# A spectral filter's rows dealt over other partitions, with a divided first load and copies made by DMA, in a one-core GFNet and GEGLU kernel

## The chip, the core and the metric

The kernel runs on one core of a Trainium2 chip. The metric is the device time of one execution in microseconds (us), the median of a few runs. Before the change it is 485.1 us (three runs, 485.1 to 485.33).

## The reference

What is computed is one block of a network: a layernorm, a filter in the frequency domain (GFNet) with a residual, a second layernorm, and a gated feed-forward part with a residual. Sequence 2048, features 576, hidden width 4608, all inputs bf16.

```python
def _A_ref(x, w_r, w_i):                      # x: 1 x 2048 x 576
    X = jnp.fft.rfft2(x.astype(jnp.float32), axes=(-2, -1))
    X = X * (w_r + 1j * w_i)                  # w_r, w_i: 2048 x 289
    return jnp.fft.irfft2(X, s=(S, D), axes=(-2, -1)).astype(jnp.bfloat16)

def _B_ref(x, w_gate, w_up, w_down):
    return (_gelu(x @ w_gate) * (x @ w_up)) @ w_down

h = x + _A_ref(_layernorm(x), A_w_r, A_w_i)
h2 = h + _B_ref(_layernorm(h), B_w_gate, B_w_up, B_w_down)
```

The change is in how the filter `w_r + 1j * w_i` gets into the on-chip memory (SBUF).

## The kernel before, in words

All matmuls are on TensorE (PE). VectorE (DVE) and ScalarE (ACT) move results out of PSUM and do the elementwise work, GpSimd (POOL) and SyncE (SP) issue DMA transfers; POOL does some elementwise work too. The order of each engine's instructions is written out by hand in strings (`SEQ1`, `SEQF`, `SEQ`), and a small scheduler (`Prog`) puts a semaphore wait in front of an instruction for each thing that it reads or overwrites. Each engine works through its own list in order.

The stages, with the times of the profiled execution:

- **Up to about 19 us**: x is loaded (2304 KB), normalised, and taken through a first DFT over 128 of the 2048 positions (`a_mm`, L551).
- **The filter stage, about 19 to 44 us** (`SEQF`). The spectrum is worked on in 16 steps i = 0 to 15; step i has the filter group `GORD[i]` = 1, 2, ... 15, 0. For each step: `D`/`d` is a DFT over the features (L640), moved out as tile `CUS`; `B` a DFT over 16 positions (L660), moved out as `YS` (there are three `YS` buffers); `T` (`st_T`, L673) multiplies `YS` with the filter tile `WS`, two DVE instructions to `TP` and `TR`; `V`/`v` and `R`/`r` (L681, L698) are the first inverse DFT, moved out as `V` and `RB`, and `RB` is spread into `VR` by small DMAs. The list begins `D2 D0 d2 D1 d0 d1 B2 D5 B0 d5 T2 D3 B1 d3 D4 T0 T1 B5 d4 D8 ...`. DVE makes the moves of `d1`, `d8`, `B1` and `B7`, ACT the other moves of `d` and `B`. So DVE's own order here is d1, T2, B1, T0, T1, d8, T3, T5, T4, T6, ...
- **About 43 to 55 us** (`SEQ`): the rest of the inverse transform (`I`, L835 and `N`, L852), the residual and the second layernorm.
- **From there to the end**: the feed-forward part, which is matmuls back to back (L944 and L1044).

**The filter tile.** `WS` is 128 partitions x 2 halves `jp` x 2 planes `pl` (0: w_r, 1: w_i) x 16 groups x 289 values. Half `jp` is loaded from HBM into the 64 partitions from 64·jp on alone: 32 of them hold "up" rows and 32 hold "down" rows (the mirrored frequencies, whose group order is reversed). Then the same 64 rows are copied to the other 64 partitions (`dup_w`), so that every partition has both halves. `st_T` of a step waits for these copies: `dup[0]` for steps 0 to 4, `dup[1]` for steps 5 to 7, `dup[2]` for steps 8 to 11, `dup[3]` from step 12 on.

- `w_up(pl, hf)` (L449) loads the up rows of a plane: two DMAs (jp = 0, 1) of 32 partitions, each row one run. `hf` 0 is groups 0 to 8 (162.6 KB a DMA), `hf` 1 groups 9 to 15 (126.4 KB).
- `w_down(pl, hf, sls, eng, sem)` (L456) loads the down rows: four DMAs (sl = 0 to 3) of 16 partitions, in runs of 578 bytes (72.2 or 63.2 KB each).
- `w_zero(pl)` (L464) loads group 0 of the down rows, two DMAs of 18.1 KB.
- SP issues, in this order: the loads of x and of tables, then for plane 1 and then plane 0 `w_up` and `w_down` of half 0 (12 DMAs), the table `VT`, the same for half 1, except that the last two `w_down` of plane 0 are issued by POOL, then `w_zero`.
- `dup_w(k, jp, pl, eng)` (L719) copies. k = 0 is groups 1 to 5, k = 1 groups 6 to 8, k = 2 groups 9 to 12, k = 3 groups 13 to 15 and 0. For k = 0, plane 1 is copied by two POOL instructions (L730) and plane 0 by two DVE instructions (L728); the others are DMAs which POOL issues. Copies of k = 0 and 1 wait for the loads of half 0, those of k = 2 and 3 for half 1.
- After the last copy SP loads the tables `VT2`, `DT`, `IT` (`tab_load`), and after them some of the `VR` pieces.
- The tables `BTAB` and `VTAB` (L140 to L152) hold the DFT coefficients in the same order of rows as `WS`; q there is the partition within a half, `half` is up or down, `r` the row, `sl` the slot.

Of the kernel before, what the change touches and what calls it, by code (L numbers as in the profile page):

```python
# [7 lines left out]
ALU = mybir.AluOpType  # L8

S, D, K2 = 2048, 576, 289  # L10
# [5 lines left out]
NT = 16  # L16
# [30 lines left out]
def build_tables():  # L47
# [52 lines left out]
    for st in range(2):  # L100
        g = 1 - st
        for p in range(128):
            half, r, jj = p // 64, (p % 64) // 4, p % 4
            low = (g + 16 * jj) if half == 0 else _minus_rows(g)[jj]
            k = 128 * r + low
            w = np.exp(-2j * np.pi * ((k * nn) % 2048) / 2048.0)
            if low in (0, 64):
                sl, ri = 0, (0 if low == 0 else 1)
# [8 lines left out]
            if half == 0:  # L117
                sl = jj
                e = np.exp(-2j * np.pi * ((r * nn) % 16) / 16.0)
                ca, cb = e, 1j * e  # L120
            else:
                sl = (128 - low - g) // 16
# [17 lines left out]
    for st in range(2):  # L140
        for jp in range(2):
            for q in range(64):
                half, r, sl = q // 32, (q % 32) // 2, 2 * jp + q % 2
                jj = sl if half == 0 else (4 - sl) % 4 if st else 3 - sl
                po, cut = 64 * half + 4 * r + jj, slice(2 * jp, 2 * jp + 2)
                for m in range(2):
                    for ri in range(2):
                        BN[jp, :, :, st, m, ri, q] = B[st, m + ri, :, cut, :, po].reshape(16, 4)
                for ri in range(2):
                    VN[st, jp, ri, q, 0] = V[st, ri, po, :, :, cut].reshape(2, 16, 4)  # L150
                    VN[st, jp, ri, q, 1] = (1 - 2 * ri) * V[st, 1 - ri, po, :, :, cut].reshape(2, 16, 4)
# [7 lines left out]
    a = np.full((K2 - 1, 1), 2.0)  # L159
# [172 lines left out]
def _build(nc, A_x, A_w_r, A_w_i, B_w_gate, B_w_up, B_w_down, out):  # L332
    P = Prog(nc)
    T = build_tables()
    dram = {n: nc.inline_tensor(_np_bf16(T[n]), name="c_" + n.lower()) for n in T}
    PE, DVE, ACT, SP, POOL = "pe", "dve", "act", "sp", "pool"
# [12 lines left out]
    WS = sb.alloc("WS", [128, 2, 2, NG, K2], BF16)  # L349
# [54 lines left out]
    ATS = sb.alloc("ATS", [128, NT, 128], BF16)  # L404
# [41 lines left out]
    P.dma(SP, FT[:, :, :].rearrange("p a b -> p (a b)"), dram["FTAB"][:, :], "ft", w=["FT"])  # L446
    P.dma(SP, BT[:, :, :, :].rearrange("p a b c -> p (a b c)"), dram["BTAB"][:, :], "bt", w=["BT", "BT1"])

    def w_up(pl, hf):  # L449
        g0, g1 = ((0, 9), (9, 16))[hf]  # L450
        src = (A_w_r, A_w_i)[pl].tensor
        for jp in range(2):
            P.dma(SP, WS[64 * jp:64 * jp + 32, jp, pl, g0:g1, :].rearrange("p g k -> p (g k)"),
                  bass.AP(src, (32 * jp + g0) * K2, [[128 * K2, 16], [16 * K2, 2], [1, (g1 - g0) * K2]]), f"w{pl}{hf}", w=[("W", hf, pl, jp)])

    def w_down(pl, hf, sls=(0, 1, 2, 3), eng=SP, sem=""):  # L456
        g0, g1 = ((1, 9), (9, 16))[hf]
        src = (A_w_r, A_w_i)[pl].tensor
        for sl in sls:
            p0 = 64 * (sl // 2) + 32  # L460
            P.dma(eng, WS[p0 + sl % 2:p0 + 32:2, sl // 2, pl, g0:g1, :], bass.AP(src, (64 + 16 * (3 - sl) + 16 - g0) * K2, [[128 * K2, 16], [-K2, g1 - g0], [1, K2]]),
                  f"w{pl}{hf}{sem}", w=[("W", hf, pl, 2 + sl)])

    def w_zero(pl):  # L464
        for jp in range(2):
            P.dma(SP, WS[64 * jp + 32:64 * jp + 64, jp, pl, 0, :], bass.AP((A_w_r, A_w_i)[pl].tensor, (64 + 32 * jp) * K2, [[128 * K2, 16], [(-16 if jp else 48) * K2, 2], [1, K2]]),
                  f"wz{pl}", w=[("W", 2, pl, jp)])

    for pl in (1, 0):
        w_up(pl, 0)  # L470
        w_down(pl, 0)
    P.dma(SP, VT[:, 0:2, :, :].rearrange("p a b c -> p (a b c)"), dram["VTAB"][:, 0:512], "vt", w=["VT", "VT1"])
    for pl in (1, 0):
        w_up(pl, 1)
        w_down(pl, 1, (0, 1, 2, 3) if pl else (0, 1))
    for pl in (1, 0):
        w_zero(pl)
    GORD = list(range(1, NG)) + [0]
    wkeys = [[("W", hf, pl, h) for pl in range(2) for h in range(6 if hf < 2 else 2)] for hf in range(3)]

# [98 lines left out]
    for w in SEQ1:  # L581
        a = w[1:]
# [9 lines left out]
    for t, w in enumerate(SEQF):  # L592
        k, i = w[0], w[1:].rstrip("abc")
        if k in "DBVR":
            b = min((b for b in used if b not in busy), key=lambda b: used[b])
# [4 lines left out]
        elif k in "dvr":  # L600
            b = FB[k.upper(), int(i)]
# [16 lines left out]
                op = mm(h, o, seqs[h][j], not second and j == 0, second and j == len(seqs[0]) - 1, [prev[o]] if second and j == 0 else [])  # L618
                turn_over.setdefault(key, [None, None])[o] = op

    dup = [[("Wd", 0, jp, pl, 1) for jp in range(2) for pl in range(2)]] + [[("Wd", k, jp, 0, g) for jp in range(2) for g in ((6,), (9,), (13, 0))[k - 1]] for k in range(1, 4)]

    wdv = B_w_down[:, :].rearrange("(c p) d -> p c d", p=128)

# [91 lines left out]
                src = PS[32 * j:32 * j + 32, b0 * 512:(b0 + 2) * 512].rearrange("p (a c) -> p a c", a=2)[:, :, 128 * (i == LAST) + 64 * t_:128 * (i == LAST) + 64 * t_ + 64]  # L716
                ev((ACT, DVE, DVE, ACT)[j], dst, src, keys, [("V", g, 2 + t_)])

    def dup_w(k, jp, pl=slice(0, 2), eng=None):  # L719
        a, b = 64 * jp, 64 - 64 * jp  # L720
        n = ("Wd", k, jp, pl.start)
        for g0, g1 in (((1, 6),), ((6, 9),), ((9, 13),), ((13, 16), (0, 1)))[k]:
            dst, src = (WS[q:q + 64, jp, pl, g0:g1, :].rearrange("p a g k -> p a (g k)")[:, :, 1:] for q in (b, a))
            r = [x for x in (wkeys[1] if g0 > 8 else wkeys[0] if g0 else wkeys[0] + wkeys[2]) if pl.start <= x[2] < pl.stop]
            if eng is None:
                op = P.dma(POOL, dst, src, f"wd{k}{jp}", r=r, w=[(*n, g0)])
            elif eng == DVE:
                P.op(DVE, lambda v: v.tensor_copy(dst, src), r=r, w=[(*n, g0)])  # L728
            else:
                P.op(POOL, lambda v: v.tensor_scalar(dst, src, 1.0, 1.0, op0=ALU.mult, op1=ALU.mult), r=r + [("ATS", NT - 1)], w=[(*n, g0)])  # L730
        return op if eng is None else None

    w_down(0, 1, (2, 3), POOL, "p")
    for jp in range(2):
        dup_w(0, jp, slice(1, 2), POOL)
        dup_w(0, jp, slice(0, 1), DVE)
    for jp in range(2):
        dup_w(1, jp)
    c = 0
    while c < NT:  # L740
        c1 = c + 1
        while c not in ACT_TILES and c1 < NT and c1 not in ACT_TILES:
            c1 += 1
        src, f, keys = (SA[:, 0, c:c1], -1.0 / D, "SA0") if c in ACT_TILES else (MV1[:, c:c1, 0], -1.0, "MV1")
        P.op(POOL, lambda g, c=c, c1=c1, src=src, f=f: g.tensor_scalar(NM[:, c:c1], src, f, 1.0, op0=ALU.mult, op1=ALU.mult),
             r=[(keys, k) for k in range(c, c1)], w=[("NM", k) for k in range(c, c1)])
        c = c1
    for k in (2, 3):
        for jp in range(2):
            last = dup_w(k, jp)  # L750
    def hold(eng=SP):
        P.op(eng, None, after=[P.ops[PE][-1]])

# [55 lines left out]
    SLOT, last, held, ing = {}, [sorted(used.values()).index(used[2 * b]) - 4 for b in range(4)], set(), False  # L809
    for t, w in enumerate(SEQ):  # L810
        k, i = w[0], int(w[1:].rstrip("ADSP"))
        if k in "INu":
            b = min((b for b in range(2 * ing, 4) if b not in held), key=lambda b: last[b])
# [3 lines left out]
        elif k in "ioUEae":  # L817
            b = SLOT[{"i": "I", "o": "N", "U": "u", "E": "I", "a": "N", "e": "u"}[k], i] // 2
# [145 lines left out]
    for w in SEQ:  # L964
        a = w[1:]
# [53 lines left out]
    for j, c in enumerate(range(NPRE, NT)):  # L1019
        f = DEF0 + DSTEP * j  # L1020
# [77 lines left out]
def bass_sequential_preLN__spectral_gfnet__geglu_ffn__prompt_kernel(  # L1098
    nc, A_x, A_w_r, A_w_i, B_x, B_w_gate, B_w_up, B_w_down, out
):  # L1100
    _build(nc, A_x, A_w_r, A_w_i, B_w_gate, B_w_up, B_w_down, out)
# [28 lines left out]
```

## Time and profile before

| what | us |
|---|---|
| median of three runs | 485.1 |
| the profiled execution's own time | 486.04 |
| its span, first to last instruction | 484.2 |
| PE busy | 477.1 (99% of the span) |
| DVE busy | 182.8 (38%) |
| ACT busy | 145.4 (30%) |
| POOL busy | 53.2 (11%) |
| last load of half 0, plane 0, issued by SP | 13.77 |
| its landing | 20.36 |
| first `T` instruction on DVE (step 2) | 22.15 |
| first `I` matmul | 43.36 |
| first feed-forward matmul (L944) | 55.54 |

How to read the profile: L242 is the line of the scheduler that issues a DMA, so all of them bear that line and one goes by their tiles (`WS<-in_A_w_r_dram` is a load, `WS<-WS` a copy). "SPq" and "POOLq" are the issuing instructions. A DMA's "us to landing" counts from the start of its issue until its last part has arrived. In a list of instructions the first number is the start and the second the time until the end of the last one of the group; brackets give the idle time of the engine just before. In the table by windows the two last columns are the mean busy share of the core's 16 DMA engines and the bytes that they moved. PE is nearly always busy over the whole span, but that says little of the 25 us of the filter stage, in which PE, ACT and DVE pass tiles to each other.

### The profile page before, as it was taken

The page shows a single profiled execution, that of the slowest core. Times are in us where ns is not written, and L with a number is a line of the kernel's source. Part 1 is how long each engine was busy: PE and PEld are TensorE (multiplying, and loading weights), DVE is VectorE, ACT ScalarE, POOL GpSimd, SP SyncE. Part 2 cuts the span into 40 slices and gives each one's busy share as a digit, 9 for nine tenths or more (in the row PEclk, how much of TensorE's full clock was granted, in tenths as well). Part 3 has the DMA queues.
Part 4 walks back from the last instruction along what each step waited for, and adds up shares of the span by engine and source line. Part 5 has one row for each costly group of instructions (what it writes and reads, how often), then busy time and mean ns, then how long its engine had stood idle before and what let it go on. Part 6 is the DMA issues. An engine that isn't in the chain of part 4 may idle for free.

```text
span 484.2 us, 12888 instructions
## 1 busy us (share of the span) xinstructions
PE 477.1 (99%) x5874; PEld 279.1 (58%) x5874; DVE 182.8 (38%) x365; ACT 145.4 (30%) x291; POOL 53.2 (11%) x88
## 2 busy tenths in 40 slices
PE   7999999999999999999999999999999999999998
PEld 4877765544577644444677544444777444444774
DVE  7988755665500144333200234333101233333011
ACT  6998753434300032233200133223100133223000
POOL 7862317010120000000000000000000000000000
PEclk9999999999999999999999999999999999999999
DMA  8955789931430001000000011000000000000000
GB/s 289 217 134 161 249 283 346 333 87 24 161 111 27 26 15 23 20 1 0 3 14 15 26 24 22 14 0 2 3 14 26 14 1 0 1 1 1 3 26 26
DMA packets 28438, 33.19 MB, mean 69 GB/s; under 512 B 12624, under 2 KB 21472, under 8 KB 28384
## 3 DMA queue, kind: packets, MB, share of 16 engines
q1 hardware_dynamic: 24720, 19.87, 14.5%
q0 software_dynamic: 3664, 12.50, 8.0%
q8 instruction: 46, 0.75, 0.7%
q14 instruction: 8, 0.07, 0.1%
HBM read 26.21 MB, written 2.36 MB: 59 GB/s over the span
## 4 chain that ended last, share of the span: by engine, by line
PE 91%; SPq 3%; DMA 2%; DVE 2%; ACT 1%; issue 0%; DVEq 0%
PE PS L944 58%; PE PS L1044 27%; SPq L242 3%; PE PS L1056 2%; DMA WS<-in_A_w_r_dram 1%; PE PS L640 1%; DMA VR<-RB 1%; PE PS L994 1%; DVE XO L858 1%; PE PS L681 1%; ACT YS L606 1%; PE PS L835 0%; PE PS L660 0%; PE PS L1011 0%; PE PS L852 0%
## 5 line engine op out<-in xcount | busy, mean ns | idle before, releaser
L944 PE MATMUL PS<-HT,WG 64*128 64x512 bf16 (+1 forms) x2142 | 233.3, 372 | 0.1
L944 PEld LDWEIGHTS PS<-HT,WG 64*128 64x128 bf16 x2142 | 105.8, 94 | 114.5 <-DVE AT L953 0.2
L952 ACT ACTIVATE GL<-PS 128x512 bf16<-128x512 f32 x144 | 85.7, 596 | 281.7 <-PE PS L944 281.7
L953 DVE TENSOR_TENSOR AT<-GL,PS 128x512 bf16<-128x512 bf16 x144 | 98.8, 687 | 166.0 <-ACT GL L952 166.0
L1044 PE MATMUL PS<-WD,AT 64*128 64x288 bf16 x2160 | 132.9, 283 | 0.0
L1044 PEld LDWEIGHTS PS<-WD,AT 64*128 64x128 bf16 x2160 | 102.5, 94 | 30.6
L1031 DVE TENSOR_TENSOR OS<-PS,XO 128x288 bf16<-128x288 f32 (+2 forms) x32 | 13.3, 453 | 125.5 <-PE PS L1044 118.0
L944 PE MATMUL PS<-HT,WGX 64*128 64x512 bf16 x486 | 53.4, 376 | 0.0
L944 PEld LDWEIGHTS PS<-HT,WGX 64*128 64x128 bf16 x486 | 23.0, 94 | 29.4
L861 ACT ACTIVATE OS<-XO,NM 128x576 bf16<-128x576 bf16 x15 | 11.6, 774 | 11.4 <-DVE XO L1015 11.4
L640 PE MATMUL PS<-FT,U 64*128 64x288 bf16 x160 | 13.7, 284 | 0.3 <-DVE V L606 0.2
L673 DVE TENSOR_TENSOR TP<-YS,WS 128x1024 bf16<-128x1024 bf16 x16 | 11.0, 688 | 1.0 <-PE PS L698 1.0
L494 DVE BATCH_NORM_STATS2 ST<-XO 128x6 f32<-128x288 bf16 x26 | 10.1, 442 | 1.9 <-DMA XO<-in_A_x_dram 1.8
L681 PE MATMUL PS<-VT,TP 64*128 64x128 bf16 x256 | 10.0, 217 | 0.0
L242 POOL DMA_DIRECT2D WG<-in_B_w_gate_dram x9 | 6.1, 679 | 32.2 <-DMA WG<-in_B_w_gate_dram 28.9
L562 ACT ACTIVATE U<-PS 128x384 bf16<-128x384 f32 (+2 forms) x27 | 9.4, 479 | 0.7 <-PE PS L551 0.7
L242 POOL DMA_DIRECT2D WD<-in_B_w_down_dram x9 | 6.7, 755 | 26.1 <-PE PS L1011 26.1
L551 PE MATMUL PS<-ATS,XO 128*128 128x128 bf16 x96 | 8.3, 219 | 1.4 <-POOL ATS L520 1.4
L606 ACT ACTIVATE CUS<-PS 128x576 bf16<-128x576 f32 x14 | 9.0, 654 | 0.7 <-PE PS L640 0.5
L606 ACT ACTIVATE YS<-PS 128x576 bf16<-128x576 f32 x14 | 8.9, 653 | 0.6 <-PE PS L660 0.4
L1056 PE MATMUL PS<-WD,AT 128*128 128x448 bf16 (+1 forms) x72 | 9.0, 286 | 0.0
L681 PEld LDWEIGHTS PS<-VT,TP 64*128 64x128 bf16 x256 | 8.0, 94 | 1.3
(89 smaller groups left out, 230.0 us busy)
## 6 DMA issues: line engine op xcount, KB each, us to landing
WD<-in_B_w_down_dram POOLq DMA_DIRECT2D x9, 576.0 KB, 10.7
WG<-in_B_w_up_dram SPq DMA_DIRECT2D x6, 576.0 KB, 6.4
WG<-in_B_w_gate_dram POOLq DMA_DIRECT2D x6, 576.0 KB, 5.7
out_dram<-OS SPq DMA_DIRECT2D x30, 72.0 KB, 1.7
XO<-in_A_x_dram SPq DMA_DIRECT2D x6, 288.0 KB, 4.5
WGX<-in_B_w_up_dram SPq DMA_DIRECT2D x2, 576.0 KB, 4.7
WGX<-in_B_w_gate_dram POOLq DMA_DIRECT2D x2, 576.0 KB, 5.8
HT<-HN SPq DMA_TRANSPOSE x60, 2.4
```

Of the source, the lines that this page charges most:

```text
L242: fn = lambda e: e.dma_start(out_ap, in_ap)
L606: fn = (lambda v: v.tensor_copy(dst, src)) if eng == DVE else (lambda a: a.activation(dst, src, ACTF.Copy))
L640: return P.op(PE, lambda t: t.matmul(bank(b0 + o, 0, 128, 0, 2 * HK), U[64 * h:64 * h + 64, us, 2 * i:2 * i + 2, :, :], FT[64 * h:64 * h + ...
L673: P.op(DVE, lambda v, dst=dst, y4=y4, w4=w4: v.tensor_tensor(dst, y4, w4, op=ALU.mult), r=[("Y", sl), *dup[(i >= 5) + (i >= 8) + (i >= 12) ...
L681: return P.op(PE, lambda t: t.matmul(bank(b0 + o, 0, 128, 128 * c, 128 * c + 128), TP[64 * h:64 * h + 64, z, o, t_, c:256:2], VT[64 * h:64 ...
L861: P.op(ACT, lambda a, c=c, out=out: a.activation(out, XO[:, c, 0:D], ACTF.Square, bias=NM[:, c:c + 1], accum_out=SB2[:, 1, c:c + 1]), r=[( ...
L944: op = P.op(PE, lambda t, h0=h0, kt=kt, wt=wt, b=b, s=(not second and j == 0), e=(second and j == n - 1): t.matmul(bank(b, 0, 128, c0, c1) ...
L952: P.op(ACT, lambda a: a.activation(GL[:, s2, :], bank(b0), ACTF.Gelu_apprx_tanh), r=[("PS", b0)], w=[("GL", s2)])
L953: P.op(DVE, lambda v: v.tensor_tensor(AT[:, f, :], GL[:, s2, :], bank(b0 + 1), op=ALU.mult), r=[("GL", s2), ("PS", b0 + 1)], w=[("AT", f)])
L1031: P.op(DVE, lambda v: v.tensor_tensor(OS[:, p % 2, d0:d1], bank(b, 0, 128, 0, d1 - d0), XO[:, c, d0:d1], op=ALU.add), r=[("PS", b), ("X", ...
L1044: e[h] = P.op(PE, lambda t, f=f, h=h, r0=r0, j=j: t.matmul(bank(b0 + h, 0, 128, 0, 288), AT[r0:r0 + 64, f, 128 * p:128 * p + 128], WD[r0:r ...
L1056: P.op(PE, lambda t, b=b, d0=d0, d1=d1, f=f, j=j: t.matmul(bank(b, 0, 128, 0, d1 - d0), AT[:, f, 128 * p:128 * p + 128], WD[:, f, d0:d1], ...
```

## The change

- **The rows dealt anew.** In each half's 64 partitions the up rows were in the first 32 and the down rows in the last 32. Now partition q of a half is: row q // 4, slot 2·jp + (q // 2) % 2, up if q is even and down if odd. Loads, `w_zero` and the two tables follow.
- **The first piece divided.** The first DMA of all, up rows of plane 1, half 0, jp = 0, is cut in two: rows 0 to 7 at first (16 partitions, 8 outer rows in the source; in the change's own words it is split over 8 of the DMA engines), and rows 8 to 15 after all other loads of half 0, ahead of `VT`, on a semaphore of its own.
- **All by SP.** The two `w_down` pieces that POOL issued are issued by SP, at their place in half 1.
- **Copies of groups 1 to 5 as transfers.** The two POOL instructions (L730) and the two DVE instructions (L728) are gone. In their place POOL issues two DMAs, jp = 0 and 1, of both planes at once. Each k has one semaphore for its DMAs.

```diff
-                half, r, sl = q // 32, (q % 32) // 2, 2 * jp + q % 2
+                half, r, sl = q % 2, q // 4, 2 * jp + q // 2 % 2
...
-    def w_up(pl, hf):
+    def w_up(pl, hf, jp, r0=0, r1=16):
...
-            P.dma(SP, WS[64 * jp:64 * jp + 32, jp, pl, g0:g1, :].rearrange("p g k -> p (g k)"),
-                  bass.AP(src, (32 * jp + g0) * K2, [[128 * K2, 16], [16 * K2, 2], [1, (g1 - g0) * K2]]), f"w{pl}{hf}", w=[("W", hf, pl, jp)])
+        P.dma(SP, WS[64 * jp + 4 * r0:64 * jp + 4 * r1:2, jp, pl, g0:g1, :].rearrange("p g k -> p (g k)"),
+              bass.AP(src, (128 * r0 + 32 * jp + g0) * K2, [[128 * K2, r1 - r0], [16 * K2, 2], [1, (g1 - g0) * K2]]), f"w{pl}{hf}" + "b" * (r0 > 0), w=[("W", hf, pl, 6 if r0 else jp)])
...
+        jp, p0 = sl // 2, 64 * (sl // 2) + 2 * (sl % 2) + 1
+        P.dma(SP, WS[p0:64 * jp + 64:4, jp, pl, g0:g1, :], bass.AP(src, (64 + 16 * (3 - sl) + 16 - g0) * K2, [[128 * K2, 16], [-K2, g1 - g0], [1, K2]]),
+              f"w{pl}{hf}", w=[("W", hf, pl, 2 + sl)])
...
+    def w_half(pl, hf):
+        w_up(pl, hf, 0, 0, 16 - 8 * (pl > hf))
+        w_up(pl, hf, 1)
+        for sl in range(4):
+            w_down(pl, hf, sl)
+
+    w_half(1, 0)
+    w_half(0, 0)
+    w_up(1, 0, 0, 8, 16)
     P.dma(SP, VT[:, 0:2, :, :].rearrange("p a b c -> p (a b c)"), dram["VTAB"][:, 0:512], "vt", w=["VT", "VT1"])
+    w_half(1, 1)
+    w_half(0, 1)
...
-    def dup_w(k, jp, pl=slice(0, 2), eng=None):
+    def dup_w(k):
...
+            for jp in range(2):
+                a, b = 64 * jp, 64 - 64 * jp
+                dst, src = (WS[q:q + 64, jp, :, g0:g1, :].rearrange("p a g k -> p a (g k)")[:, :, 1:] for q in (b, a))
+                op = P.dma(POOL, dst, src, f"wd{k}", r=wkeys[1] if g0 > 8 else wkeys[0] if g0 else wkeys[0] + wkeys[2], w=[("Wd", k, jp, g0)])
+        return op
+
+    dup_w(0)
+    dup_w(1)
```

More of the change, by code (lines that the diff above doesn't have):

```diff
@@ L447, in _build @@
     P.dma(SP, BT[:, :, :, :].rearrange("p a b c -> p (a b c)"), dram["BTAB"][:, :], "bt", w=["BT", "BT1"])
-    def w_up(pl, hf):
+    def w_up(pl, hf, jp, r0=0, r1=16):
         g0, g1 = ((0, 9), (9, 16))[hf]
         src = (A_w_r, A_w_i)[pl].tensor
-        for jp in range(2):
-            P.dma(SP, WS[64 * jp:64 * jp + 32, jp, pl, g0:g1, :].rearrange("p g k -> p (g k)"),
-                  bass.AP(src, (32 * jp + g0) * K2, [[128 * K2, 16], [16 * K2, 2], [1, (g1 - g0) * K2]]), f"w{pl}{hf}", w=[("W", hf, pl, jp)])
@@ L456, in w_down @@
-    def w_down(pl, hf, sls=(0, 1, 2, 3), eng=SP, sem=""):
+        P.dma(SP, WS[64 * jp + 4 * r0:64 * jp + 4 * r1:2, jp, pl, g0:g1, :].rearrange("p g k -> p (g k)"),
+              bass.AP(src, (128 * r0 + 32 * jp + g0) * K2, [[128 * K2, r1 - r0], [16 * K2, 2], [1, (g1 - g0) * K2]]), f"w{pl}{hf}" + "b" * (r0 > 0), w=[("W", hf, pl, 6 if r0 else jp)])
+    def w_down(pl, hf, sl):
         g0, g1 = ((1, 9), (9, 16))[hf]
         src = (A_w_r, A_w_i)[pl].tensor
[L459 to L462, printed above, removed]
+        jp, p0 = sl // 2, 64 * (sl // 2) + 2 * (sl % 2) + 1
+        P.dma(SP, WS[p0:64 * jp + 64:4, jp, pl, g0:g1, :], bass.AP(src, (64 + 16 * (3 - sl) + 16 - g0) * K2, [[128 * K2, 16], [-K2, g1 - g0], [1, K2]]),
+              f"w{pl}{hf}", w=[("W", hf, pl, 2 + sl)])
@@ L464, in w_zero @@
     def w_zero(pl):
         for jp in range(2):
-            P.dma(SP, WS[64 * jp + 32:64 * jp + 64, jp, pl, 0, :], bass.AP((A_w_r, A_w_i)[pl].tensor, (64 + 32 * jp) * K2, [[128 * K2, 16], [(-16 if jp else 48) * K2, 2], [1, K2]]),
+            P.dma(SP, WS[64 * jp + 1:64 * jp + 64:2, jp, pl, 0, :], bass.AP((A_w_r, A_w_i)[pl].tensor, (64 + 32 * jp) * K2, [[128 * K2, 16], [(-16 if jp else 48) * K2, 2], [1, K2]]),
                   f"wz{pl}", w=[("W", 2, pl, jp)])
-    for pl in (1, 0):
-        w_up(pl, 0)
-        w_down(pl, 0)
+    def w_half(pl, hf):
[3 more added lines that the diff above has]
+            w_down(pl, hf, sl)
@@ L472, in _build @@
+    w_half(1, 0)
+    w_half(0, 0)
+    w_up(1, 0, 0, 8, 16)
     P.dma(SP, VT[:, 0:2, :, :].rearrange("p a b c -> p (a b c)"), dram["VTAB"][:, 0:512], "vt", w=["VT", "VT1"])
-    for pl in (1, 0):
-        w_up(pl, 1)
-        w_down(pl, 1, (0, 1, 2, 3) if pl else (0, 1))
+    w_half(1, 1)
+    w_half(0, 1)
     for pl in (1, 0):
@@ L478, in _build @@
     GORD = list(range(1, NG)) + [0]
-    wkeys = [[("W", hf, pl, h) for pl in range(2) for h in range(6 if hf < 2 else 2)] for hf in range(3)]
+    wkeys = [[("W", hf, pl, h) for pl in range(2) for h in range((6 + (pl > hf)) if hf < 2 else 2)] for hf in range(3)]
     def act_sum(c):
@@ L619, in halves @@
                 turn_over.setdefault(key, [None, None])[o] = op
-    dup = [[("Wd", 0, jp, pl, 1) for jp in range(2) for pl in range(2)]] + [[("Wd", k, jp, 0, g) for jp in range(2) for g in ((6,), (9,), (13, 0))[k - 1]] for k in range(1, 4)]
+    dup = [[("Wd", k, jp, g) for g in ((1,), (6,), (9,), (13, 0))[k] for jp in range(2)] for k in range(4)]
     wdv = B_w_down[:, :].rearrange("(c p) d -> p c d", p=128)
@@ L717, in st_R @@
                 ev((ACT, DVE, DVE, ACT)[j], dst, src, keys, [("V", g, 2 + t_)])
-    def dup_w(k, jp, pl=slice(0, 2), eng=None):
-        a, b = 64 * jp, 64 - 64 * jp
-        n = ("Wd", k, jp, pl.start)
+    def dup_w(k):
         for g0, g1 in (((1, 6),), ((6, 9),), ((9, 13),), ((13, 16), (0, 1)))[k]:
[L723 to L738, printed above, removed]
+            for jp in range(2):
[5 more added lines that the diff above has]
+    dup_w(1)
     c = 0
@@ L747, in _build @@
         c = c1
-    for k in (2, 3):
-        for jp in range(2):
-            last = dup_w(k, jp)
+    dup_w(2)
+    last = dup_w(3)
     def hold(eng=SP):
```

## The prediction

> **What bounds the kernel now.** I read the page first: where is PE idle? Its last 420 us are matmuls back to back, which this change does not touch, so what counts is how late they begin (55.54 us). Then the chain of waits between 13 and 29 us, when the filter arrives:
>
> ```profile
> 13.77 6.59 DMA WS<-in_A_w_r_dram
> 20.36 0.02 issue
> 20.38 0.53 DVE WS L728
> ...
> 20.92 0.54 DVE WS L728
> 21.46 0.03 DVEq L307
> 21.50 0.63 DVE CUS L606
> 22.13 0.05 issue
> 22.18 0.42 PE PS L640 x4
> ```
>
> The end was set here by the last load of half 0 (6.59 us from issue, landed at 20.36), then by the two DVE copies, then by a DVE move that had stood behind them. So the landing of the filter is on the path, and so is whatever comes between it and the first multiplication. DVE's own list shows what follows:
>
> ```profile
> 20.38 1.07 DVE L728 COPY WS<-WS 64x1444 bf16<-64x1444 bf16 x2 [1.05 <-DMA WS<-in_A_w_r_dram]
> 21.37 0.75 DVE L606 CAST CUS<-PS 128x576 bf16<-128x576 f32 x1
> 22.15 0.69 DVE L673 TENSOR_TENSOR TP<-YS,WS 128x1024 bf16<-128x1024 bf16 x1
> ...
> 27.51 0.70 DVE L673 TENSOR_TENSOR TP<-YS,WS 128x1024 bf16<-128x1024 bf16 x1 [0.95 <-PE PS L698]
> ```
>
> The first T (step 2) begins at 22.15. After it DVE hardly rests: by the windows it works 20.46 of the 22 us from 22 to 44, and 0.95 of the 1.54 us of rest is the gap before T5. Its label names PE, but st_T(5) waits for `dup[1]`, and the second copy of groups 6 to 8 was issued at 21.58 and took 5.8 us: 27.4. It is a DMA that ends this gap. Next, what the DMA engines do:
>
> ```profile
> 6.00:8.00 2.00, 1.10 (x16) 0.78 (x15) 2.00 (x9) 0.66 (x4) 1.53 (x4) 1.00 0.91 343
> 14.00:16.00 2.00, 2.00 (x37) 1.86 (x35) 2.00 (x9) 2.00 (x8) 1.76 (x3) 1.00 1.10 228
> 18.00:20.00 2.00, 2.00 (x36) 1.66 (x35) 1.29 (x4) 1.78 (x7) 1.92 (x2) 1.00 1.08 201
> 24.00:26.00 2.00, 2.00 (x40) 1.34 (x37) 2.00 (x6) 1.97 (x4) 1.17 (x3) 1.00 0.92 153
> 29.00:31.00 2.00, 2.00 (x43) 1.71 (x42) 2.00 (x7) 1.61 (x4) 2.00 (x5) 1.00 0.88 202
> ```
>
> The last two columns are DMA share and GB/s. Busy throughout, they moved 343 GB/s while x came to 128 partitions, but 201 to 228 while filter rows came to 64 partitions of one half at a time; 153 with copies and loads mixed; 202 with copies alone. Last the waits, SP's own and the other engines' (total, times, longest):
>
> ```profile
> SPq L242 <- DMA WS<-WS: 5.1, 1, 5.1
> ```
>
> ```profile
> POOL WS L242 <- DMA WS<-in_A_w_r_dram: 2.9, 2, 2.5
> PE PS L835 <- DMA VR<-RB: 0.6, 1, 0.6
> ```
>
> SP stood 5.1 us for the last copy, POOL twice for loads before it could issue copies; PE, at the end of the stage, 0.65 us for a piece of VR that shared the DMA engines with the tables that SP loaded after the last copy. PE's granted clock was 1.00 in every window.
>
> **Part 1, the loads of half 0.** The bytes are the same: 2 x (2 x 162.6 + 4 x 72.2) = 1228 KB. What is new is that, if the piece runs on 8 engines as the change says, these begin with jp = 0 while the others go straight to jp = 1, and from then on the two groups may write to different halves. If that does nothing, the landing moves little: 8 engines carry two rows of 9 x 578 bytes, 10.4 KB, more than their mean, at 224 GB/s / 16 (mean of 12 to 20 us) +0.74 us; POOL's two pieces, 126 KB that ran beside them, are gone, at 208 GB/s (16 to 20 us) -0.6 us: 20.5. If filter rows flow at x's 343, 1228 KB take 3.6 instead of 5.5 us: 18.6. SP's issues are the floor: one more of 0.64 us puts the last issue at 14.4, and no WS DMA landed in under 2.9 us: 17.3. I take 18.6, the row of transfers to both halves at once.
>
> [...]
>
> **Part 2, copies of groups 1 to 5.** Gone: two DVE copies (1.07 us) and two POOL instructions of 1.39 us. POOL's cost was hidden: it ran beside A's last matmuls and before the landing. DVE's 1.07 lay on the path. Added: two DMAs of 64 x 2 x 2888 B = 361 KB, 722 KB in all, on POOL's queue behind the landing of half 0, ahead of the copies of groups 6 to 8. They read the SBUF and write it, so there is no row of just this; the nearest are the other WS copies:
> - Alone: first issue at 27.89; the second of two 288.8 KB copies, issued at 28.55, took 4.5, so 578 KB landed 5.2 us after the first issue; the four behind them (577 KB) were all there at 36.1, 3.0 us later, 190 KB per us. 722 KB: 5.2 + 145/190 = 5.9 us.
> - Beside loads: first issue at 20.64; the two of 216.5 KB landed at 26.1 and 27.4, 6.8 us for 433 KB, the second 1.3 us after the first (166 KB per us). 722 KB: 6.8 + 289/166 = 8.5 us.
>
> SP goes on issuing half 1 until about 26 + 0.64 + 2 x 0.6 = 28 us, all through this, so the mixed row is nearer: I take 7.5. POOL itself is free by then (its last XN ends at 16.1) and issued 0.28 us after the old landing. The copies land at 18.6 + 0.3 + 7.5 = **26.4**; the ends are 17.3 + 0.3 + 5.9 = 23.5 and 20.5 + 0.3 + 8.5 = 29.3.
>
> **Part 3, who waits.** The new wait is that of T2 on DVE, the first user of `dup[0]`. Without it T2 could begin at 21.9, when ACT's YS is there (21.21 + 0.65). It begins at 26.4 instead of 22.15: +4.25. Behind it on DVE stand the move of B1, T0, T1, d8. ACT waits too: its move of B5 writes the YS buffer that T2 reads, so after d5 and d3 it stands, and PE soon has no free PSUM. So little is done ahead, and the rest of the stage moves as one. What comes off:
> - The gap before T5, 0.95 us: the copies of groups 6 to 8 follow by 433/166 = 2.6 us, at 29.0, and T5 is due 4.4 us after T2, at 30.8. Hidden now; uncovered again if they need over 4.4 us.
> - Of DVE's other rests (0.6 us together), some 0.2.
> - PE's 0.65 us for VR: tables start when the last copy lands, about when they did (36.1), so 3 us of delay in RB takes the last pieces out of their way. What is late next there is the move of V and VR on DVE and ACT, 44.4 plus the delay.
>
> Copies for step 8 and on: half 1 lands later by SP's three extra issues, 1.8 us at most, and T8 had 34.38 - 33.06 = 1.3 us of slack; T8 is itself 3 us later, so nothing. The new semaphores and `w_zero` cost nothing: no engine waits there. Tables and `w_zero` with other rows have the same sizes.
>
> **Sum:** +4.25 - 0.95 - 0.2 - 0.65 = **+2.45 us**, say +2.4 (with 23.5: -0.45; with 29.3: +5.35). On the profiled execution, span 484.2 and own time 486.04 with 1.84 around it, that is a span of 486.6 and 488.5; the median of the runs, 485.1, is 0.94 below that execution, and so I forecast 485.1 + 2.4 = 487.5.
>
> **The rivals.**
> 1. *Both halves run at once, copies too, and T2 does not wait* (no change, or faster). For it: 343 GB/s was had when both halves were written. Against it: a copy reads one half and writes the other, all 16 engines the same way, and had 202 alone. Place: T2. It decides when the copies land by about 22: with the landing at 17.3, 722 KB at 343 GB/s (2.1 us), POOL's 0.3 and 1.1 from issue to first packet (27.89 to 29.0) they land at 20.8. Then T2 gains 0.25, T5 0.95 and VR up to 0.65, 1.85 at most; I take -1.3, 483.8, as ACT's moves from 22 to 44 (23.6 us, overlapping) are as full as DVE's. Copies that land at 23.5 give 484.7, no change. Chances 0.13 and 0.14.
> 2. *The divided piece does nothing, the copies run as beside loads* (slower still). The cut then only moves half a piece to the end of the list: landing 20.5, copies 29.3, +5.35: 490.4. [...] Chance 0.15. [...]
> 3. The forecast: loads faster, copies late, 486.1 to 489.6, about 487.5. Chance 0.58.
>
> So slower by over 0.2% (0.97 us, about what a measurement of this kernel can tell from no change) 0.73, within it 0.14, faster 0.13. The range, 484.6 to 490.4, is the sum's own; it leaves out the faster half of rival 1 (0.13) and half of rival 2 (0.07).
>
> **What would show it.** In the profile after: the last load of half 0 landing at 17.3 to 19.5 and GB/s over 300 between 12 and 18 us (part 1); no L728 or L730; two WS<-WS DMAs of 361 KB with 6 to 8.5 us to landing (part 2); DVE idle 3 us or more before its first L673, which starts near 26.4, with a DMA WS<-WS as the releaser, no gap before T5, first L835 near 46 and first L944 near 58 (part 3). I am wrong if the first T starts before 23, or if it starts late and L944 does not: then DVE was not what the stage hangs on.

## The result and the profile after

The changed kernel takes 492.06 us (median of four runs, 491.53 to 492.75) against 485.1 (four runs, 484.55 to 485.33): 1.0146 times as long, interval 1.0127 to 1.0165. That is slower, as forecast, but by 7.0 us and not by 2.4, and above the range. The profiled execution of the changed kernel took 491.54 us, its span is 489.7.

The chain of waits in the changed kernel, over the same stretch as before (start, us, what):

```profile
14.36 4.75 DMA WS<-in_A_w_i_dram
...
19.18 0.61 issue
19.80 0.83 POOL WS L242
20.64 6.73 DMA WS<-WS
27.39 0.69 DVE TP L676
...
30.08 1.20 PE PS L643 x10
```

The last load of half 0 is now the second part of the divided piece; it lands at 19.12, 1.24 us sooner than before's last load (20.36). Then POOL needs 0.68 us to its first issue, and the copies 7.57 us from there (19.80 to 27.37). T2 begins at 27.39 instead of 22.15. From the last landing to T2 it is 8.3 us now; before it was 1.8, of which the two DVE copies were 1.07.

The last row is one that no row of before prepared for: ten matmuls of the feature DFT take 1.20 us, 120 ns each. In the same kernel, some microseconds later, the chain has ten of them in half of that:

```profile
35.40 0.61 PE PS L643 x10
```

DVE's own list in the changed kernel, and who waited for whom from 19 to 52 us (total, times, longest):

```profile
27.39 0.69 DVE L676 TENSOR_TENSOR TP<-YS,WS 128x1024 bf16<-128x1024 bf16 x1 [5.55 <-DMA WS<-WS]
...
32.91 0.70 DVE L676 TENSOR_TENSOR TP<-YS,WS 128x1024 bf16<-128x1024 bf16 x1 [0.56 <-PE PS L684]
```

```profile
DVE TP L676 <- DMA WS<-WS: 5.6, 1, 5.6
...
PE PS L643 <- DVE YS L609: 5.0, 1, 5.0
ACT YS L609 <- DVE TR L676: 4.5, 1, 4.5
```

The three waits are one: DVE for the copies, ACT for T2 (its move of B5 overwrites the `YS` that T2 reads), PE for the move behind T2 that frees its PSUM. PE stood from 23.93 to 28.94. What that did to PE shows in its row by windows (window, its length, PE busy and matmuls, granted clock, DMA share, GB/s):

```profile
27.00:28.00 1.00, 0.00 (x0) 1.00 1.11 180
28.00:29.00 1.00, 0.06 (x2) 0.58 0.95 140
29.00:30.00 1.00, 1.00 (x10) 0.50 0.50 78
30.00:31.00 1.00, 1.00 (x12) 0.50 0.07 18
31.00:32.00 1.00, 1.00 (x17) 0.71 0.00 0
32.00:33.00 1.00, 1.00 (x34) 1.00 0.59 125
```

The granted clock was 1.00 throughout before. Here it falls to 0.50 at 28.17, 4.2 us into PE's stand, and stays there for 3.4 us, 10 to 17 matmuls a microsecond instead of 34. (In another trace, `e7_half1_held` in the last section, PE was already at work again when the fall came.) This is what the prediction lacked: behind this stand PE worked at half the clock for 2.6 us, 28.94 to 31.58.

The sum, step by step on the profiled executions (spans 484.2 and 489.7):

| | before | after | change | forecast |
|---|---|---|---|---|
| first T (step 2) begins | 22.15 | 27.39 | +5.24 | +4.25 |
| from there to T of step 15 (40.89; 47.00) | 18.74 | 19.61 | +0.87 | -1.15 |
| from there to the first `I` matmul (43.36; 49.47) | 2.47 | 2.47 | 0 | 0 |
| from there to the first feed-forward matmul (55.54; 61.06) | 12.18 | 11.59 | -0.59 | -0.65 |
| from there to the end of the span | 428.66 | 428.64 | -0.02 | 0 |
| sum | | | +5.50 | +2.45 |

The rest of the 7.0 us lies in the choice of executions: before's profiled one was 0.94 above its median, that of after 0.52 below.

### The profile page after: what moved, and what is told of

Read it like the earlier page. It is cut to its first block, busy times and chain, and to the rows that moved or that the text cites. A ratio compares the mean times of both kernels' runs of the same rounds, so it can differ in the third digit from the quotient of the medians.

```text
span 489.7 us, 12887 instructions
## 1 busy us (share of the span) xinstructions
PE 477.6 (98%) x5874; PEld 279.6 (57%) x5874; DVE 182.1 (37%) x363; ACT 145.4 (30%) x291; POOL 49.0 (10%) x86
## 4 chain that ended last, share of the span: by engine, by line
PE 92%; SPq 3%; DMA 2%; DVE 1%; issue 1%; POOL 0%; POOLq 0%; DVEq 0%
PE PS L937 57%; PE PS L1037 27%; SPq L242 3%; PE PS L1049 2%; PE PS L684 2%; PE PS L643 1%; DMA WS<-WS 1%; DMA WS<-in_A_w_i_dram 1%; PE PS L663 1%; PE PS L828 1%; PE PS L987 1%; DVE XO L851 1%; PE PS L1004 0%; PE PS L845 0%; PE PS L701 0%
## 5 line engine op out<-in xcount | busy, mean ns | idle before, releaser
L854 ACT ACTIVATE OS<-XO,NM 128x576 bf16<-128x576 bf16 x15 | 11.6, 773 | 11.4 <-DVE XO L1008 11.4
L643 PEld LDWEIGHTS PS<-FT,U 64*128 64x128 bf16 x160 | 7.2, 98 | 7.7 <-DVE YS L609 5.3
```

Of the source, the lines that this page charges most:

```text
L643: return P.op(PE, lambda t: t.matmul(bank(b0 + o, 0, 128, 0, 2 * HK), U[64 * h:64 * h + 64, us, 2 * i:2 * i + 2, :, :], FT[64 * h:64 * h + ...
L854: P.op(ACT, lambda a, c=c, out=out: a.activation(out, XO[:, c, 0:D], ACTF.Square, bias=NM[:, c:c + 1], accum_out=SB2[:, 1, c:c + 1]), r=[( ...
```

## The experiments

**1. The changed kernel with the old copies** (`e1_new_loads_old_copies`). Loads as changed; groups 1 to 5 are copied by POOL and DVE again.

```diff
-    dup_w(0)
-    dup_w(1)
+    for jp in range(2):
+        dup_w(0, jp, slice(1, 2), POOL)
+        dup_w(0, jp, slice(0, 1), DVE)
+    for jp in range(2):
+        dup_w(1, jp)
...
```

> The changed kernel with one part undone: groups 1 to 5 are copied by two GpSimd and two VectorE instructions again, so rows, divided piece and SP's loads are those of the change. Theory (the first T waits for the two 361 KB copies, all else is small): loads of half 0 land at 19.1 as in the changed kernel, VectorE copies at about 19.4, GpSimd copies plane 1 from 19.2 to 22.0, the first T starts at 21.9 to 22.3 instead of 27.39, PE's clock stays at 1.00, and the time is 484.0 to 486.0, that of the kernel before or a little under. Rival A (the new rows, the divided piece or SP's three extra issues cost the time): the first T is early and the time still lies over 489. Rival B (the piece's gain of 1.2 us in landing comes through): under 484.3.

Measured: 486.01 us, ratio 1.0007 (0.9998 to 1.0017). The loss is gone, and no gain is left. Half 0 landed at 18.30, 2 us sooner than before, yet T2 began at 23.09, 0.8 us later than expected; `I` at 43.64, the feed-forward part at 55.80. DVE's list in this kernel, and POOL's:

```profile
20.19 2.21 DVE L731 COPY WS<-WS 64x1444 bf16<-64x1444 bf16 x2
```

```profile
18.43 2.86 POOL L733 TENSOR_SCALAR WS<-WS 64x1444 bf16<-64x1444 bf16 x2 [1.52 <-DVE U L565]
```

POOL's two copies need the whole of plane 1, and the end of plane 1 is now the second part of the divided piece. So they ran from 18.43 to 21.29 (17.44 to 20.30 before), into DVE's. Those took 1.49 and 0.70 us instead of 0.53 each. The 2 us won on the loads were lost to that, and to DVE's moves of `U`, which kept it until 20.2 (19.3 before: this execution was 0.8 us behind from its first DFT matmul on, 8.06 against 7.23). DVE's first copy took about as long as if it had run only once POOL's were done: from 20.19 to 21.29 is 1.1 us of wait, with 0.53 behind it about 1.6, and 1.49 was measured. That is an estimate from these rows; what held DVE's copy up is not shown. In the four other profiles where the two met, the same working is also 0.14 us above what DVE's first copy took. Why the second copy took 0.70, with POOL's done, is not shown either.

**2. The kernel before with only the copies changed** (`e5_copies_only`). Loads as before, and the two 361 KB DMAs for groups 1 to 5.

```diff
-        dup_w(0, jp, slice(1, 2), POOL)
-        dup_w(0, jp, slice(0, 1), DVE)
+        dup_w(0, jp)
```

> The kernel before with one part of the change: groups 1 to 5 are copied by two DMAs of 361 KB; rows, pieces and GpSimd's two loads stay as before. Theory: the loads land at 20.4 as before, the copies 8.3 us later as in the changed kernel, 28.6, the first T starts there, PE stands 6 us and its clock halves for 3 us or more; the time is 1 to 2 us over the changed kernel's 492.1: 492.5 to 494.5. Rival A (loads or rows cost it, not the copies): within 1 us of 485.1. Rival B (the copies are slow because SP issues more beside them): they land within 6.5 us of the loads, and the time is 488 to 490.

Measured: 492.23 us, ratio 1.0138 (1.0121 to 1.0154): the whole loss of the change, from this one edit. Half 0 landed at 19.54, not at 20.4, and the time is 0.3 us under the expected range. First issue 19.82, copies landed at 28.12, 8.3 us later and 8.6 behind the loads, so rival B is refuted too. DVE's list and the windows of this kernel (PE, PEld, DVE, ACT, POOL busy, granted clock, DMA share, GB/s):

```profile
28.20 0.69 DVE L673 TENSOR_TENSOR TP<-YS,WS 128x1024 bf16<-128x1024 bf16 x1 [6.50 <-DMA WS<-WS]
```

```profile
26.00:28.00 2.00, 0.00 (x0) 0.00 (x0) 0.00 (x0) 0.00 (x0) 0.00 (x0) 0.77 1.02 211
28.00:30.00 2.00, 0.25 (x4) 0.16 (x6) 1.80 (x4) 0.94 (x2) 0.00 (x0) 0.50 0.54 68
```

The same wait of DVE and the same halved clock. From 26 to 28 us PE, DVE, ACT and POOL all stood, while the DMA engines were busy throughout at 211 GB/s.

**3. The parts of the loads, one by one** (`e2_no_divided_piece`, `e3_rows_as_before`, `e4_all_by_sp`). All keep the old copies. The first takes the division of the piece out of experiment 1, the second its new rows (both diffs are against experiment 1); the third is the kernel before with only POOL's two loads moved to SP.

```diff
-        w_up(pl, hf, 0, 0, 16 - 8 * (pl > hf))
+        w_up(pl, hf, 0, 0, 16)
...
-    w_up(1, 0, 0, 8, 16)
...
```

> As e1 (rows dealt anew, all loads by SP, copies of groups 1 to 5 by GpSimd and VectorE), but the first piece is not divided. Plane 1 then lands whole at about 17 again, GpSimd copies it from there, ahead of VectorE's copies, and these take 1.1 us together as in the kernel before instead of 2.2 in e1, where both copied at once. Theory (neither rows nor piece matter to the loads, GpSimd and VectorE hinder each other when they copy together): loads of half 0 land at 19.0 to 19.8, the first T at 21.8 to 22.2, time 484.6 to 485.6. Rival (the divided piece lets the two halves of the memory be written at once): the loads land at 20 or later and the time is over 486.

```diff
-                half, r, sl = q % 2, q // 4, 2 * jp + q // 2 % 2
+                half, r, sl = q // 32, (q % 32) // 2, 2 * jp + q % 2
...
-        P.dma(SP, WS[64 * jp + 4 * r0:64 * jp + 4 * r1:2, jp, pl, g0:g1, :].rearrange("p g k -> p (g k)"),
+        P.dma(SP, WS[64 * jp + 2 * r0:64 * jp + 2 * r1, jp, pl, g0:g1, :].rearrange("p g k -> p (g k)"),
...
```

> As e1, with the divided piece and all loads by SP, but the rows dealt as before. Theory (the rows do nothing): as e1, loads of half 0 at 18.8 to 19.6, VectorE's copies 2 us because GpSimd copies beside them, time 485.5 to 486.5. Rival (the piece needs the new rows, so that each engine meets its own part of the memory): landing 0.7 us or more later than with the new rows, 20.0 or more, and the time over 486.7.

```diff
-    w_down(0, 1, (2, 3), POOL, "p")
...
+    w_half(1, 1)
+    w_half(0, 1)
...
```

> The kernel before with one part of the change: SP issues the two loads of half 1 that GpSimd issued. Theory: these two no longer run beside half 0's loads, which land up to 0.6 us sooner, 19.0 to 19.8; the copies of groups 6 to 8 still end the wait of T5; time 484.6 to 485.6, within the noise of the kernel before. Rival (SP's two extra issues hold up half 1 and its copies): the time rises by 0.5 us or more, and T8 waits for a copy.

| | us, ratio | half 0 lands | T2 | first `I` |
|---|---|---|---|---|
| `e1_new_loads_old_copies` | 486.01, 1.0007 (0.9998 to 1.0017) | 18.30 | 23.09 | 43.64 |
| `e2_no_divided_piece` | 485.66, 1.0019 (1.0007 to 1.0031) | 18.96 | 21.81 | 42.34 |
| `e3_rows_as_before` | 486.88, 1.0042 (1.0027 to 1.0057) | 21.35 | 24.48 | 45.72 |
| `e4_all_by_sp` | 485.7, 1.0011 (1.0001 to 1.0020) | 18.07 | 22.07 | 42.58 |

With the old rows the divided piece costs time, as the rival in `e3_rows_as_before` had it (its reason, which part of the memory an engine meets, is not shown): half 0 lands some 2.5 us later than with the new rows, POOL's copy of plane 1 can begin only then (21.49), T2 waits for that copy, and the kernel is 0.42% slower. With the new rows the piece gains nothing that shows in the time over loading all by SP with the old rows undivided. None of the four is faster than before. In `e2_no_divided_piece` the stretch from `I` to the feed-forward part was 13.2 us (11.6 to 12.2 elsewhere): PE waited 1.6 us there for a DMA `VR<-RB`, 0.65 in the kernel before. Why that piece came so late is open.

**4. PE kept busy during the wait** (`e6_keep_busy`). The changed kernel with 44 matmuls of zeros after d4, into columns that nothing reads; the moves of B5 and d4 are listed behind them. They add work that the result does not need.

```diff
+            for _ in range(44):
+                P.op(PE, lambda t: t.matmul(bank(b5, 0, 128, 288, 512), ZD[:, 0:128], ZD[:, 0:224], start=True, stop=True), r=["ZD"], w=[("PS", b5)])
+            for held in late:
+                ev(*held)
...
```

> The changed kernel, with 44 matmuls of zeros (into columns of a PSUM bank that nothing reads) put where PE stands from 23.9 to 28.9; nothing else moves. They take about 4.2 us. Theory (the halved clock after the stand costs time of its own, on top of the late T): the granted clock stays at 1.00 from 28 to 32, the first T starts at 27.4 as before, T5 no longer waits for PE, and the time is 0.9 to 1.5 us under the changed kernel, 490.5 to 491.2, with the executions closer together than its 491.5 to 492.8. Rival (VectorE sets the stage, PE's clock is hidden): clock 1.00, and the time within 0.3 us of the changed kernel's.

Measured: 490.22 us (489.47 to 491.12), ratio 1.0097 (1.0078 to 1.0115); its interval lies below that of the change. The windows of this kernel:

```profile
26.00:28.00 2.00, 2.00 (x23) 1.86 (x20) 0.39 (x1) 0.00 (x0) 0.00 (x0) 1.00 1.04 207
28.00:30.00 2.00, 0.96 (x16) 0.61 (x16) 2.00 (x6) 1.26 (x3) 0.00 (x0) 1.00 0.87 111
30.00:32.00 2.00, 1.97 (x46) 1.47 (x44) 2.00 (x5) 1.78 (x4) 0.48 (x1) 1.00 0.11 19
```

The clock stays at 1.00. The copies landed no sooner (27.59, T2 at 27.61), yet from T2 to T of step 15 it takes 18.02 us, where the changed kernel took 19.61, and the gap before T5 is gone:

```profile
32.06 0.70 DVE L681 TENSOR_TENSOR TP<-YS,WS 128x1024 bf16<-128x1024 bf16 x1
```

So the halved clock cost 1.6 us by this stretch, 1.8 by the medians, 2.4 by the ratios (0.0049 of 485). The two moves were reordered with it, although the expectation says that nothing else moves; the run does not separate that from the matmuls. The time is 0.3 us under the expected range, and the executions were no closer together (1.65 us from lowest to highest, 1.22 in the changed kernel). What is left is 0.97%. The profile has it as the lateness of T2: 5.46 us, less 0.72 to T of step 15 and 0.58 behind the first `I`, is 4.2, the difference of the spans (488.4 and 484.2).

**5. The copies with no loads beside them** (`e7_half1_held`). The changed kernel, but SP issues half 1 only after the two 361 KB copies have landed.

```diff
+    P.op(SP, None, after=[dup_w(0)])
+    dup_w(1)
+    w_half(1, 1)
+    w_half(0, 1)
```

> The changed kernel, but SP issues the loads of half 1 and of group 0 only when both 361 KB copies have landed. Theory (the copies take 7.6 us from first issue because they share the DMA engines with half 1's loads): alone they land 5.9 us after their first issue, at about 25.7, the first T starts there, 1.7 us sooner; half 1 then lands at about 34 and its copies at 38 to 40, so that T8 is no sooner than 39 and may wait; the time is 489 to 493. Rival (the copies are slow by themselves, whatever runs beside them): the first T stays at 27.0 or later, and the time rises by the lateness of half 1 alone.

Measured: 494.92 us (two runs), ratio 1.0192 (1.0169 to 1.0216), above the expected 489 to 493. First issue 19.06, both copies there at 25.68, 6.6 us later. That the landing came where it was expected is luck: the copies took 0.7 us more than the 5.9 forecast and began 0.7 us sooner than in the changed kernel.

```profile
25.70 0.69 DVE L672 TENSOR_TENSOR TP<-YS,WS 128x1024 bf16<-128x1024 bf16 x1 [4.07 <-DMA WS<-WS]
...
42.43 0.69 DVE L672 TENSOR_TENSOR TP<-YS,WS 128x1024 bf16<-128x1024 bf16 x1 [3.69 <-DMA WS<-WS]
```

Beside loads it was 7.6 (the changed kernel) to 8.3 (`e5_copies_only`), so the loads cost it 1.0 to 1.7 us, and without them it takes 6.6. (The 433 KB of groups 6 to 8 were copied behind these two in every run, here until 26.63; no run has the two alone.) The second row shows what holding half 1 back costs: T8 now waits 3.7 us for its copies, PE stands a second time, for 3.4 us, and its clock falls a second time; the kernel loses more than it won. An estimate from these rows: 6.6 us of copies behind the earliest landing seen, 18.0, and POOL's 0.3 put T2 at 24.9 at best, not at 22, while 722 KB are copied by DMA.

**6. Repeats** (`e8_changed_again`, `e9_before_again`, `e10_all_by_sp_again`, `e11_rows_as_before_again`), the same kernels as the change, before, experiments `e4_all_by_sp` and `e3_rows_as_before`. The question was how far landings read from one execution repeat.

> The changed kernel again, beside the others on one chip, for its spread and its clock. Theory (PE stands 5 us, and how long its clock then stays at half differs from one execution to the next): times in two groups, about 491.5 and 492.7, the mean granted clock 0.997 and 0.993; the first T at 27.2 to 27.7 in either. Rival (the spread is the copies' landing): the first T differs by about 1 us between executions of either group.

> The kernel before, a second profiled execution, to see how much its landing of half 0 differs between executions; in the first it was 20.36 and the execution was 0.9 us slower than the median. Theory (GpSimd's two pieces run beside half 0 in every execution): landing 19.5 to 20.5, first T 21.9 to 22.3, first feed-forward matmul 54.2 to 55.6. Rival (the first landing was a slow exception): under 19.2, as with all loads by SP.

> The kernel of e4 again, a second profiled execution. Theory (SP issuing all loads is what brings half 0 sooner): landing 18.0 to 19.2 again, first T 21.9 to 22.3. Rival (spread between executions): 19.5 or later.

> The kernel of e3 again (divided piece, rows as before), a second profiled execution; in the first the divided piece's last part landed at 21.35. Theory (the divided piece on 8 engines with the old rows makes pairs of engines meet on the same part of the memory): 20.5 or later again, first T over 23.5. Rival (a slow exception): 18.0 to 19.2, as with the new rows.

| | us | half 0 lands | T2 |
|---|---|---|---|
| changed; again | 492.06; 491.78 | 19.12; 18.01 | 27.39; 26.36 |
| before; again | 485.1; 485.17 | 20.36; 19.84 | 22.15; 21.93 |
| all by SP; again | 485.7; 485.95 | 18.07; 19.84 | 22.07; 22.94 |
| rows as before; again | 486.88; 487.48 | 21.35; 20.90 | 24.48; 24.06 |

The changed kernel repeats (ratio 1.0145, 1.0127 to 1.0164). My idea that its executions differ by the clock alone fell: in the second profile T2 is 1.0 us sooner, but the clock is low for longer, T2 to T15 takes 20.24 us, and the end is the same within 0.4 us; nor do its four times fall into two groups with two clocks (491.14 and 493.28 both had 0.993). Landings of one kernel differ by up to 1.8 us between executions (0.7 of it because one execution issued its loads that much later), so the differences between `e1_new_loads_old_copies`, `e2_no_divided_piece` and `e4_all_by_sp` prove nothing; the late landing with the divided piece and old rows came both times.

## Why the prediction was right in sign and too small

- **Part 1, the loads (right in the landing, wrong in the reason).** 18.6 was forecast; the five profiles with new rows and division gave 18.0 to 19.1. But the sign that was to show it, over 300 GB/s from 12 to 18 us, did not come. The windows of the changed kernel give 318, 235 and 200; before they were 250, 228 and 216:

```profile
12.00:14.00 2.00, 1.92 (x35) 1.92 (x36) 2.00 (x10) 2.00 (x9) 1.51 (x4) 1.00 1.13 318
14.00:16.00 2.00, 2.00 (x37) 1.90 (x35) 2.00 (x10) 2.00 (x7) 1.76 (x3) 1.00 1.06 235
16.00:18.00 2.00, 2.00 (x39) 2.00 (x37) 2.00 (x10) 2.00 (x7) 0.34 (x1) 1.00 0.80 200
```

  From 14 us on, when x and the tables ahead of the rows have landed (the last at 13.66), the rows do not run at x's rate, 343 in the kernel before; from 16 us on the DMA engines are not even full (0.80). So the number came right by luck. Moving POOL's two loads behind half 0, with the old rows and no division, gave 18.07 and 19.84. Counted from the first `WS` issue of the same execution, half 0 took 13.1 to 14.0 us in the three profiles with before's loads, 11.9 to 13.0 in the three with all loads by SP and no division, and 11.8 to 12.9 in the five with the new rows and the division. So about 1 us goes with POOL's two loads, and what could be due to the rows and the division, 0.3 by the means, lies within the spread.
- **Part 2, the copies (right).** 7.5 us from the first issue were forecast, 7.57 measured (7.97 in the second profile), between 6.6 without loads and 8.3; the ends had been 5.9 and 8.5, so the lower one was 0.7 too low. They landed at 27.37 instead of 26.4 because the loads landed 0.5 later and POOL took 0.68 us, not 0.3, to its first issue. That is +1.0 of the sum.
- **Part 3, who waits: this is the step that failed.** The chain DVE, ACT, PE was right, and so was the releaser. But the prediction let "the rest of the stage" move "as one" and took 1.15 us off for gaps that would close. It had noted that PE "soon has no free PSUM" and had read a granted clock of 1.00 everywhere, and did not ask what a stand of 5 us would do to that clock: the term was put at nothing without a reason. T2 to T15 took 0.87 us more instead of 1.15 less, 2.0 of the sum; with PE kept busy (`e6_keep_busy`) it took 0.72 less than before's first profile and 0.17 less than its second.
- **The base.** The gap before T5 that was taken off, 0.95 us, was in part that execution's own: before's second profile, 0.87 us faster, has 0.41 there, labelled with the DMA that the prediction had named, and 18.19 from T2 to T15. By these two profiles some 0.5 us was taken off twice, as a gap that closes and again within the 0.94 of going from the profiled execution to the median. The two distances from the medians, 0.94 and after's own 0.52, are 1.5 of the missing 4.6; 1.0 lies in part 2 and 2.0 in part 3.
- **The tail (right).** PE's wait of 0.65 for VR went, -0.59.
- **The rivals.** Rival 1, copies that are in time, was refuted: T2 waited in every run with the DMA copies. Rival 2 came closest in time (490.4), but not in its mechanism: loads landed 1.4 us and the copies 1.9 us before its times.

## What to carry to other kernels

A copy on the path is priced from its first issue to its landing, with what else the DMA engines carry at that time: two DVE copies of 0.53 us were replaced by a transfer of 6.6 to 8.3 us. When a wait will stop TensorE for some microseconds (in these traces 3.4 were enough, 2.1 were not), add the slower clock after it as a term of its own, here 1.6 to 2.4 us, on top of the wait. And do not subtract a gap seen in one execution and that execution's distance from the median as well.

## What the hardware showed that was not expected

- The granted clock fell to 0.50 in every trace in which PE stood for 3.4 us or more (3.4 and 3.5 in `e7_half1_held`, 4.2 in `e8_changed_again`, 5.0 in the changed kernel, 6.0 in `e5_copies_only`) and in none in which it stood for 2.1 or less (2.1 in `e3_rows_as_before`). The fall came 2.4 to 4.6 us after PE had stopped, in `e7_half1_held` when PE was already at work again: of the 3.41 us before the first fall, as long as the clock was low behind it, PE was busy for 0.89, and of as many before the second for 1.21. Here are the 3.41 us before and behind the first one (PE's windows):

```profile
24.73:28.14 3.41, 0.89 (x16) 1.00 0.48 149
28.14:31.55 3.41, 3.41 (x48) 0.50 0.52 131
```

- The clock stayed low for 3.4 us in the first profile of the changed kernel and both times in `e7_half1_held`, and for twice that, 6.8, in `e5_copies_only` and in the second profile of the changed kernel, although PE began again a microsecond sooner there. So 2.6 to 5 us of the work behind the stand ran at half the clock. PE's windows of `e8_changed_again`:

```profile
26.12:29.53 3.41, 1.61 (x14) 0.50 0.63 141
29.53:32.94 3.41, 3.41 (x46) 0.50 0.57 103
33.00:34.00 1.00, 1.00 (x36) 1.00 0.94 235
```

- DVE's copy of 64x1444 took 0.53 us by itself and 0.8 to 1.49 when it began while POOL copied from SBUF to SBUF (`e1_new_loads_old_copies`, `e2_no_divided_piece`, both profiles of all by SP, the second profile of before). A load that lands sooner can bring two engines together that were apart.
- Open: why the divided piece with the old rows lands late. By the code each of its two parts then writes 16 neighbouring partitions, with the new rows every second one of 32. The expectations' guess, that DMA engines meet on the same part of the memory, is not shown: the traces do not tell which engine carried what, and no run settled it.
